# A SwiGLU feed-forward kernel: the first 256 rows of x loaded as row pairs, and the first gate weights issued from another queue

## The chip, the cores and the metric

The kernel runs on one core of a Trainium2 chip. The metric is device time in microseconds (us), from launch to end. The profile is one execution taken by the hardware profiler; its "span" runs from the core's first to its last instruction. PE is TensorE (PEld its weight loads), ACT is ScalarE, DVE is VectorE, POOL is GpSimd, and SP is SyncE, which only issues DMA here. DMA issued from SP is seen in the profile as queue q1, from ACT as q10, from POOL as q0.

## What is computed

x has 2048 rows of 640, the gate and up weights are 640 x 1536, the down weight is 1536 x 640, all bf16:

```
g = silu(x @ w_gate)
u = x @ w_up
out = (g * u) @ w_down
```

## The kernel before

The rows of x are worked on in four blocks of 512 (`S_BLK`), and the 1536 columns of the hidden layer in 12 pieces of 128 (`KF`, index `fc`). The contraction of 640 is 5 pieces of 128 (`KD`, index `kd`). In a block, each `fc` has five matmuls into `pg` (gate) and five into `pu` (up); ACT applies Silu from `pg`, DVE multiplies with `pu` and writes the hidden activations, transposed, into `aT`. When the 12 pieces are done, the down projection runs in two parts: output columns 512 to 639 come from one group of 12 matmuls `po_t`, with the 512 rows of the block as the moving side, so that they come out transposed; and columns 0 to 511 come from four groups `po_a`, one for each 128 rows `j`. `po_t` is copied by ACT to `ot_t` (L283), turned by DVE in 32x32 squares (L285) and stored from ACT's queue (L287). `po_a` is copied by ACT (L312) and stored from SP's queue (L321). The last four rows of x are handled apart, as row products on DVE (L148), which the change doesn't touch.

TensorE needs x with its columns on the partitions (`xT`). For most rows that is done by the DMA (`turn_x`, L110). For the first two chunks of 128 rows, `PE_X = 2`, it is done on TensorE: the rows are loaded into `x_sb` (L86), transposed against an identity (L190), and copied to `xT` by ACT (`kd` 0 and 1) and DVE (`kd` 2 to 4) (L195). Chunk 0 is loaded from SP's queue, chunk 1 from ACT's.

Behind these two loads come the first 256 columns (`fc` 0 and 1) of the gate and up weights, each in two parts, split at `K_CUT = 2`: `kd` 0 and 1 of the gate from SP, `kd` 2 to 4 of the gate from ACT, `kd` 0 and 1 of up from POOL, `kd` 2 to 4 of up from SP (L120). Then SP issues the transposing load of rows 256 to 511 and all the other weights.

`head()` writes TensorE's first work by hand, and `keep_order` keeps it so: 20 warming matmuls on a tile of ones (L177), ten transposes (five for each chunk), 14 gate matmuls (L240: for `kd` 0 and 1 first the 128 rows of chunk 0, then those of chunk 1, then `kd` 2 to 4 over both chunks' 256 rows), ten up matmuls over the same 256 rows, and then rows 256 to 511 of the same two pieces. After that the regular loop goes on with `fc` 2. Each engine works through its own instructions in the order given and waits at each for its semaphores.

Of the kernel before, what the change touches and what calls it, by code (L numbers as in the profile page):

```python
# [10 lines left out]
def _body(  # L11
# [8 lines left out]
    nc = tc.nc  # L20
    P = nc.NUM_PARTITIONS
# [8 lines left out]
    x2 = x.rearrange("b s d -> (b s) d")  # L30
    out2 = out.rearrange("b s d -> (b s) d")

    KD = D // P
    KF = F // P
    S_BLK = 512
# [7 lines left out]
    PE_X = 2  # L43
    K_CUT = 2
# [12 lines left out]
    x_sb = consts.tile([P, PE_X, D], bf16)  # L57
    xT = consts.tile([P, KD, S], bf16)
    wg_sb = consts.tile([P, KD, F], bf16)
    wu_sb = consts.tile([P, KD, F], bf16)  # L60
# [9 lines left out]

    make_identity(nc, ident[:])

    x_v = x2.rearrange("(c p) d -> p c d", p=P)
    xt_v = x2.rearrange("s (kd p) -> s kd p", p=P)
    wg_v = w_gate.rearrange("(kd p) f -> p kd f", p=P)
    wu_v = w_up.rearrange("(kd p) f -> p kd f", p=P)
    wd_v = w_down.rearrange("(kf p) d -> p kf d", p=P)

    def wslice(a, b):
        return slice(a * P, b * P)  # L80

    def load_w(eng, dst, src, a, b):
        eng.dma_start(out=dst[:, :, wslice(a, b)], in_=src[:, :, wslice(a, b)])

    def load_x(eng, c0, c1):
        eng.dma_start(out=x_sb[:, c0:c1, :], in_=x_v[:, c0:c1, :])  # L86

    def issue_order(a, b):
        tc.add_manual_dep(
# [18 lines left out]
    def turn_x(c0, c1):  # L108
        s_sl = slice(c0 * P, c1 * P)
        nc.sync.dma_start_transpose(out=xT[:, :, s_sl], in_=xt_v[s_sl])  # L110

    load_x(nc.sync, 0, 1)
    load_x(nc.scalar, 1, 2)
    f_sl = wslice(*W_CHUNKS[0])
    for dst, src, first, second in (
        (wg_sb, wg_v, nc.sync, nc.scalar),
        (wu_sb, wu_v, nc.gpsimd, nc.sync),
    ):
        for eng, k_sl in ((first, slice(0, K_CUT)), (second, slice(K_CUT, KD))):
            eng.dma_start(out=dst[:, k_sl, f_sl], in_=src[:, k_sl, f_sl])  # L120
    turn_x(PE_X, SUB)
    nc.scalar.activation(silu_first[:], ones[:, 0:1], ACT.Silu)
    for a, b in W_CHUNKS[1:]:
# [6 lines left out]
    def turn_w(dst, src):  # L130
# [7 lines left out]
        out=x_row[:],  # L138
        in_=x2[S - T : S, :].rearrange("t d -> (t d)").partition_broadcast(P),
# [29 lines left out]
    def do_dots(n):  # L169
        for _ in range(n):  # L170
            next(dots, None)
# [3 lines left out]
    def warm(n):  # L175
        for _ in range(n):
            nc.tensor.matmul(  # L177
                pw[:, 0:P],
                lhsT=ones[:].broadcast_to([P, P]),
                rhs=ones[:].broadcast_to([P, P]),  # L180
                start=True,
                stop=True,
            )

    def transpose_chunk(c, parts):
        c_sl = slice(c * P, (c + 1) * P)
        for copy, tag, k0, k1 in parts:
            pt = psum.tile([P, k1 - k0, P], bf16, tag=tag, name="pt")
            for kd in range(k0, k1):
                nc.tensor.transpose(  # L190
                    out=pt[:, kd - k0, :],
                    in_=x_sb[:, c, kd * P : (kd + 1) * P],
                    identity=ident[:],
                )
            copy(out=xT[:, k0:k1, c_sl], in_=pt[:])  # L195

    def proj(ps, w_sb, fc, sb, c0, c1):
        for kd in range(KD):
            nc.tensor.matmul(  # L199
                ps[:, c0:c1],  # L200
                lhsT=w_sb[:, kd, fc * P : (fc + 1) * P],
                rhs=xT[:, kd, sb * S_BLK + c0 : sb * S_BLK + c1],
                start=(kd == 0),
                stop=(kd == KD - 1),
            )

    def gu_tiles():
        pg = psum.tile([P, S_BLK], f32, tag="gu", name="pg", bufs=4)
        pu = psum.tile([P, S_BLK], f32, tag="gu", name="pu", bufs=4)
        return pg, pu  # L210

    def gate(pg, pu, sb, fc, n_s):

        s0 = sb * S_BLK
        sg = work.tile([P, S_BLK], f32, name="sg")
        nc.scalar.activation(sg[:, 0:n_s], pg[:, 0:n_s], ACT.Silu)  # L216
        nc.vector.tensor_tensor(  # L217
            out=aT[:, fc, s0 : s0 + n_s], in0=sg[:, 0:n_s], in1=pu[:, 0:n_s], op=ALU.mult
        )

    def head():

        dve, act = nc.vector.tensor_copy, nc.scalar.copy
        split = [(act, "po_a", 0, 2), (dve, "po_b", 2, KD)]
        late = PE_X * P
        (pg0, pu0), (pg1, pu1) = gu_tiles(), gu_tiles()  # L230
        warm(N_WARM)
        transpose_chunk(0, split)
        transpose_chunk(1, split)
        early = [(kd, c * P, (c + 1) * P) for c in range(PE_X) for kd in range(K_CUT)]
        early += [(kd, 0, late) for kd in range(K_CUT, KD)]
        for kd, c0, c1 in early:
            for fc, pg in ((0, pg0), (1, pg1)):


                nc.tensor.matmul(  # L240
                    pg[:, c0:c1],
                    lhsT=wg_sb[:, kd, wslice(fc, fc + 1)],
                    rhs=xT[:, kd, c0:c1],
                    start=(kd == 0 and c0 == 0),
                    stop=(kd == KD - 1),
                )
        proj(pu0, wu_sb, 0, 0, 0, late)
        proj(pu1, wu_sb, 1, 0, 0, late)
        for fc, pg, pu in ((0, pg0, pu0), (1, pg1, pu1)):
            proj(pg, wg_sb, fc, 0, late, S_BLK)  # L250
            proj(pu, wu_sb, fc, 0, late, S_BLK)
            gate(pg, pu, 0, fc, S_BLK)
        keep_order(mybir.EngineType.PE)
        keep_order(mybir.EngineType.Activation)
        keep_order(mybir.EngineType.Pool)

    head()
    for sb in range(NSB):
        n_s = S_BLK if sb < NSB - 1 else S_BLK - T
        for fc in range(KF):  # L260
            if sb == 0 and fc < 2:
                continue
            pg, pu = gu_tiles()
            proj(pg, wg_sb, fc, sb, 0, n_s)
            proj(pu, wu_sb, fc, sb, 0, n_s)
            gate(pg, pu, sb, fc, n_s)
            if sb > 0 and fc < KF - 2:
                do_dots(2)


        n_t = (SUB if sb < NSB - 1 else SUB - 1) * P
        po_t = psum.tile([P, n_t], f32, tag="po_b", name="po_t")
        for kf in range(KF):
            nc.tensor.matmul(  # L274
                po_t[:],
                lhsT=wd_sb[:, kf, DA:D],
                rhs=aT[:, kf, sb * S_BLK : sb * S_BLK + n_t],
                start=(kf == 0),
                stop=(kf == KF - 1),
            )  # L280
        ot_t = outp.tile([P, n_t], bf16, name="ot_t")
        ot_q = outp.tile([P, n_t], bf16, name="ot_q")
        nc.scalar.copy(ot_t[:], po_t[:])  # L283
        do_dots(3)
        nc.vector.transpose(out=ot_q[:], in_=ot_t[:])  # L285
        for q in range(P // Q):
            nc.scalar.dma_start(  # L287
                out=out2[
                    sb * S_BLK : sb * S_BLK + n_t, DA + q * Q : DA + (q + 1) * Q
                ].rearrange("(i r) c -> r i c", r=Q),  # L290
                in_=ot_q[q * Q : (q + 1) * Q, :].rearrange("r (i c) -> r i c", c=Q),
            )

        for j in range(SUB):
            s0 = sb * S_BLK + j * P
            last = sb == NSB - 1 and j == SUB - 1
            cols = [(0, DA, "po_a")]
            if last:
                cols = [(0, DA // 2, "po_a"), (DA // 2, DA, "po_a"), (DA, D, "po_b")]
            for c0, c1, tag in cols:  # L300
                po = psum.tile([P, c1 - c0], f32, tag=tag, name="po_a")
                for kf in range(KF):
                    nc.tensor.matmul(  # L303
                        po[:],
                        lhsT=aT[:, kf, s0 : s0 + P],
                        rhs=wd_sb[:, kf, c0:c1],
                        start=(kf == 0),
                        stop=(kf == KF - 1),
                    )
                ot = outp.tile([P, c1 - c0], bf16, name="ot" if c1 < D else "ot_b")  # L310
                if c1 < D:
                    nc.scalar.copy(ot[:], po[:])  # L312
                    eng = nc.sync
                else:
                    nc.vector.tensor_copy(out=ot[:], in_=po[:])  # L315
                    eng = nc.sync
                if 0 < j and not last:
                    do_dots(3)
                if sb == NSB - 1 and j == ROW_J:
                    row_tail()  # L320
                eng.dma_start(out=out2[s0 : s0 + P, c0:c1], in_=ot[:])  # L321
        if sb == 0:
            turn_x(2 * SUB, 3 * SUB)
            turn_w(wuT, wut_v)
            turn_x(3 * SUB, 4 * SUB)
# [107 lines left out]
```

## Time and profile before

| | us |
|---|---|
| median of 3 runs | 163.5 (163.18 to 163.65) |
| the profiled execution: its time | 163.61 |
| its span | 162.2 |
| PE busy (share of the span) | 159.8 (98%) |
| DVE busy | 110.8 (68%) |
| ACT busy | 42.9 (26%) |
| DMA, share of the chain that ended last | 2% |

The chain of waits is read from the last instruction backwards; in it PE has 97% of the span and the load of `x_sb` at the start has 1.7%. A busy TensorE says nothing of its pace: how many matmuls of what width went by in a stretch has to be counted. What lies around the span is 163.61 - 162.2 = 1.4 us.

### The profile page before, as it was taken

How to read it: one execution, taken by the hardware profiler on the slowest of the kernel's cores; microseconds unless marked ns; L12 is line 12 of the kernel's file. 1: busy time of each engine (PE TensorE's matmuls, PEld its weight loads, DVE VectorE, ACT ScalarE, POOL GpSimd, SP SyncE). 2: the span in 40 equal slices, each digit the busy share in tenths (PEclk: the TensorE clock that was granted, in tenths of full speed). 3: DMA queues.
4: the chain of work that ended last, by engine and by line, in shares of the span. 5: the costliest groups of instructions: out<-in, count | busy, mean ns of one | idle time of the engine just before them, and what ended most of it. 6: DMA issues, size and time to landing. Idle time of an engine off the chain costs nothing.

```text
span 162.2 us, 2119 instructions
## 1 busy us (share of the span) xinstructions
PE 159.8 (98%) x798; PEld 78.1 (48%) x798; DVE 110.8 (68%) x249; ACT 42.9 (26%) x74; POOL 1.5 (1%) x7
## 2 busy tenths in 40 slices
PE   8999999999999999999999999999999999999995
PEld 8854444444444444444444444444444444445454
DVE  1042233599469999979919999979964999993000
ACT  5132222112222222221222322221214222222121
POOL 3000000000000000000000000000000000000000
PEclk9999999999999999999999999999999999999999
DMA  7999999993179996003110000000320000000212
GB/s 215 275 343 350 363 217 220 240 216 87 35 164 161 205 177 136 4 0 34 65 65 0 0 4 2 0 0 1 63 68 33 0 0 0 0 0 4 50 39 73
DMA packets 42217, 15.86 MB, mean 98 GB/s; under 512 B 33216, under 2 KB 42048, under 8 KB 42208
## 3 DMA queue, kind: packets, MB, share of 16 engines
q1 hardware_dynamic: 33680, 14.75, 37.6%
q10 hardware_dynamic: 8480, 0.85, 3.4%
q8 instruction: 6, 0.10, 0.3%
q0 software_dynamic: 48, 0.13, 0.2%
q14 instruction: 3, 0.02, 0.1%
HBM read 6.88 MB, written 2.62 MB: 59 GB/s over the span
## 4 chain that ended last, share of the span: by engine, by line
PE 97%; DMA 2%; DVE 0%; issue 0%
PE pu L199 32%; PE pg L199 31%; PE po_a L303 26%; PE po_t L274 6%; DMA x_sb<-in_x_dram 2%; PE pg L240 1%; PE pt L190 1%; DVE ot_b L315 0%
## 5 line engine op out<-in xcount | busy, mean ns | idle before, releaser
L199 PE MATMUL pu<-xT,wu_sb 128*128 128x512 bf16 (+2 forms) x250 | 59.7, 370 | 0.0
L199 PE MATMUL pg<-xT,wg_sb 128*128 128x512 bf16 (+2 forms) x240 | 58.5, 374 | 0.0
L217 DVE TENSOR_TENSOR aT<-sg,pu 128x512 bf16<-128x512 f32 (+1 forms) x48 | 32.8, 684 | 32.4 <-PE pu L199 28.1
L216 ACT ACTIVATE sg<-pg 128x512 f32<-128x512 f32 (+1 forms) x48 | 28.6, 597 | 70.8 <-PE pg L199 66.2
L303 PE MATMUL po_a<-wd_sb,aT 128*128 128x512 bf16 (+2 forms) x216 | 42.8, 358 | 0.0
L148 DVE SCALAR_TENSOR_TENSOR prod<-wgT,x_row 128x640 f32<-128x640 bf16 x48 | 39.4, 821 | 1.1
L148 DVE SCALAR_TENSOR_TENSOR prod<-wuT,x_row 128x640 f32<-128x640 bf16 x48 | 39.4, 822 | 1.0
L199 PEld LDWEIGHTS <-wu_sb 128*128 128x128 bf16 x250 | 24.5, 98 | 27.3
L199 PEld LDWEIGHTS <-wg_sb 128*128 128x128 bf16 x240 | 23.5, 98 | 26.9
L303 PEld LDWEIGHTS <-aT 128*128 128x128 bf16 x216 | 20.7, 98 | 21.6
L312 ACT CAST ot<-po_a 128x512 bf16<-128x512 f32 (+1 forms) x17 | 9.5, 561 | 32.0 <-PE po_a L303 20.9
L274 PE MATMUL po_t<-aT,wd_sb 128*128 128x512 bf16 (+1 forms) x48 | 10.4, 366 | 0.0
L274 PEld LDWEIGHTS <-wd_sb 128*128 128x128 bf16 x48 | 4.7, 98 | 5.1
L315 DVE CAST ot_b<-po_a 128x128 bf16<-128x128 f32 x1 | 0.3, 292 | 9.9 <-PE po_a L303 9.9
L283 ACT CAST ot_t<-po_t 128x512 bf16<-128x512 f32 (+1 forms) x4 | 2.2, 559 | 11.6 <-PE po_t L274 11.6
L148 DVE DVE_READ_ACCUMULATOR prod<-wuT,x_row 128x1 f32 x48 | 4.0, 83 | 0.0
L148 DVE DVE_READ_ACCUMULATOR prod<-wgT,x_row 128x1 f32 x48 | 3.9, 82 | 0.0
L285 DVE STREAM_TRANSPOSE ot_q<-ot_t 128x512 bf16<-128x512 bf16 (+1 forms) x4 | 2.7, 678 | 1.7 <-ACT ot_t L283 1.7
L195 DVE COPY xT<-pt 128x384 bf16<-128x384 bf16 x2 | 0.7, 358 | 3.5 <-PE pt L190 3.5
L177 PE MATMUL pw<-ones 128*128 128x128 bf16 x20 | 2.3, 310 | 0.3 <-DVE ones L106 0.3
L240 PE MATMUL pg<-xT,wg_sb 128*128 128x128 bf16 (+1 forms) x14 | 2.2, 347 | 0.0
L177 PEld LDWEIGHTS <-ones 128*128 128x128 bf16 x20 | 2.0, 144 | 0.3 <-DVE ones L106 0.3
(16 smaller groups left out, 8.4 us busy)
## 6 DMA issues: line engine op xcount, KB each, us to landing
wd_sb<-in_w_down_dram SPq DMA_DIRECT2D x1, 1920.0 KB, 14.0
out_dram<-ot SPq DMA_DIRECT2D x15, 128.0 KB, 1.7
wg_sb<-in_w_gate_dram SPq DMA_DIRECT2D x2, 640.0 KB, 8.2
wu_sb<-in_w_up_dram SPq DMA_DIRECT2D x2, 640.0 KB, 8.8
x_row<-in_x_dram SPq DMA_DIRECT2D x1, 640.0 KB, 5.2
out_dram<-ot_q ACTq DMA_DIRECT2D x12, 32.0 KB, 1.9
wg_sb<-in_w_gate_dram SPq DMA_DIRECT2D x1, 320.0 KB, 4.4
wu_sb<-in_w_up_dram SPq DMA_DIRECT2D x1, 320.0 KB, 4.9
```

The source lines that it names most:

```text
L148: nc.vector.scalar_tensor_tensor(out=prod[:], in0=wT[:, fc, :], scalar=1.0, in1=x_row[:, t, :], op0=ALU.mult, op1=ALU.mult, accum_out=acc[ ...
L177: nc.tensor.matmul(pw[:, 0:P], lhsT=ones[:].broadcast_to([P, P]), rhs=ones[:].broadcast_to([P, P]), start=True, stop=True,)
L190: nc.tensor.transpose(out=pt[:, kd - k0, :], in_=x_sb[:, c, kd * P : (kd + 1) * P], identity=ident[:],)
L199: nc.tensor.matmul(ps[:, c0:c1], lhsT=w_sb[:, kd, fc * P : (fc + 1) * P], rhs=xT[:, kd, sb * S_BLK + c0 : sb * S_BLK + c1], start=(kd == 0 ...
L216: nc.scalar.activation(sg[:, 0:n_s], pg[:, 0:n_s], ACT.Silu)
L217: nc.vector.tensor_tensor(out=aT[:, fc, s0 : s0 + n_s], in0=sg[:, 0:n_s], in1=pu[:, 0:n_s], op=ALU.mult)
L240: nc.tensor.matmul(pg[:, c0:c1], lhsT=wg_sb[:, kd, wslice(fc, fc + 1)], rhs=xT[:, kd, c0:c1], start=(kd == 0 and c0 == 0), stop=(kd == KD ...
L274: nc.tensor.matmul(po_t[:], lhsT=wd_sb[:, kf, DA:D], rhs=aT[:, kf, sb * S_BLK : sb * S_BLK + n_t], start=(kf == 0), stop=(kf == KF - 1),)
L283: nc.scalar.copy(ot_t[:], po_t[:])
L285: nc.vector.transpose(out=ot_q[:], in_=ot_t[:])
L303: nc.tensor.matmul(po[:], lhsT=aT[:, kf, s0 : s0 + P], rhs=wd_sb[:, kf, c0:c1], start=(kf == 0), stop=(kf == KF - 1),)
L312: nc.scalar.copy(ot[:], po[:])
```

## The change

The 256 rows are loaded by one DMA from SP's queue. Partition p gets rows 2p and 2p+1, which lie together in memory (2560 bytes), where before it got rows p and 128+p by two DMAs of 1280 bytes a partition. So "chunk" 0 now holds the even rows among the first 256, and chunk 1 the odd ones, and so do the first 256 columns of `xT` and `aT`. The weights' parts are dealt out anew: gate `kd` 0 and 1 is ACT's first DMA, gate `kd` 2 to 4 and up `kd` 3 and 4 are SP's, up `kd` 2 is ACT's second, and up `kd` 0 and 1 stays with POOL. The order of the rows is put right at the output: in the first block ACT's copy of `po_t` is split in two, and the one for the first 256 columns writes with a stride; the stores of `po_a` for `j` 0 and 1 go to every second row.

```diff
-    load_x(nc.sync, 0, 1)
-    load_x(nc.scalar, 1, 2)
+    paired = PE_X * P
+
+    def paired_rows(ap):
+        return ap[0:paired, :].rearrange("(p c) d -> p c d", c=PE_X)
+
+    nc.sync.dma_start(out=x_sb[:], in_=paired_rows(x2))
     f_sl = wslice(*W_CHUNKS[0])
-    for dst, src, first, second in (
-        (wg_sb, wg_v, nc.sync, nc.scalar),
-        (wu_sb, wu_v, nc.gpsimd, nc.sync),
+    for eng, dst, src, a, b in (
+        (nc.scalar, wg_sb, wg_v, 0, K_CUT),
+        (nc.sync, wg_sb, wg_v, K_CUT, KD),
+        (nc.gpsimd, wu_sb, wu_v, 0, K_CUT),
+        (nc.scalar, wu_sb, wu_v, K_CUT, K_CUT + 1),
+        (nc.sync, wu_sb, wu_v, K_CUT + 1, KD),
     ):
-        for eng, k_sl in ((first, slice(0, K_CUT)), (second, slice(K_CUT, KD))):
-            eng.dma_start(out=dst[:, k_sl, f_sl], in_=src[:, k_sl, f_sl])
+        eng.dma_start(out=dst[:, a:b, f_sl], in_=src[:, a:b, f_sl])
...
-        nc.scalar.copy(ot_t[:], po_t[:])
+        plain = 0
+        if sb == 0:
+            plain = paired
+            nc.scalar.copy(
+                ot_t[:, 0:paired].rearrange("d (p c) -> d c p", c=PE_X),
+                po_t[:, 0:paired].rearrange("d (c p) -> d c p", c=PE_X),
+            )
+        nc.scalar.copy(ot_t[:, plain:n_t], po_t[:, plain:n_t])
...
+            rows = out2[s0 : s0 + P, :]
+            if s0 < paired:
+                rows = paired_rows(out2)[:, j, :]
...
-                eng.dma_start(out=out2[s0 : s0 + P, c0:c1], in_=ot[:])
+                eng.dma_start(out=rows[:, c0:c1], in_=ot[:])
```

Elsewhere the diff only renames `late` to `paired`. TensorE's matmuls, their shapes and their order are the same in both kernels.

More of the change, by code (lines that the diff above doesn't have):

```diff
@@ L71, in _body @@
     make_identity(nc, ident[:])
-    x_v = x2.rearrange("(c p) d -> p c d", p=P)
     xt_v = x2.rearrange("s (kd p) -> s kd p", p=P)
@@ L83, in load_w @@
         eng.dma_start(out=dst[:, :, wslice(a, b)], in_=src[:, :, wslice(a, b)])
-    def load_x(eng, c0, c1):
-        eng.dma_start(out=x_sb[:, c0:c1, :], in_=x_v[:, c0:c1, :])
     def issue_order(a, b):
@@ L228, in head @@
         split = [(act, "po_a", 0, 2), (dve, "po_b", 2, KD)]
-        late = PE_X * P
         (pg0, pu0), (pg1, pu1) = gu_tiles(), gu_tiles()
@@ L234, in head @@
         early = [(kd, c * P, (c + 1) * P) for c in range(PE_X) for kd in range(K_CUT)]
-        early += [(kd, 0, late) for kd in range(K_CUT, KD)]
+        early += [(kd, 0, paired) for kd in range(K_CUT, KD)]
         for kd, c0, c1 in early:
@@ L246, in head @@
                 )
-        proj(pu0, wu_sb, 0, 0, 0, late)
-        proj(pu1, wu_sb, 1, 0, 0, late)
+        proj(pu0, wu_sb, 0, 0, 0, paired)
+        proj(pu1, wu_sb, 1, 0, 0, paired)
         for fc, pg, pu in ((0, pg0, pu0), (1, pg1, pu1)):
-            proj(pg, wg_sb, fc, 0, late, S_BLK)
-            proj(pu, wu_sb, fc, 0, late, S_BLK)
+            proj(pg, wg_sb, fc, 0, paired, S_BLK)
+            proj(pu, wu_sb, fc, 0, paired, S_BLK)
             gate(pg, pu, 0, fc, S_BLK)
```

## The prediction, made before the changed kernel ran

> **What bounds the kernel now.** I read the chain of waits first, over its first 12 us and its end.
>
> ```profile
> 0.00 2.77 DMA x_sb<-in_x_dram
> 2.77 0.05 issue
> 2.81 1.25 PE pt L190 x10
> 4.06 1.99 PE pg L240 x14
> 6.05 1.09 PE pu L199 x10
> 7.14 0.55 PE pg L199 x5
> ```
>
> ```profile
> 157.96 2.32 PE po_a L303 x27
> 160.28 0.02 issue
> 160.31 0.29 DVE ot_b L315
> ```
>
> Columns: start, length, what; first the beginning, then the end. The first 2.77 us are the load of chunk 0; from 2.81 to 160.28 there is nothing but TensorE, piece after piece, with no wait between. So only two things can move the end: when TensorE starts on x, and how fast it goes. The stretches show both.
>
> ```profile
> 2.62:2.81 0.19, 0.00 (x0) 0.00 (x1) 0.00 (x0) 0.00 (x0) 0.00 (x0) 1.00 0.95 282
> 2.81:5.78 2.97, 2.97 (x24) 2.66 (x25) 0.72 (x2) 0.75 (x2) 0.00 (x0) 1.00 1.16 288
> 5.78:7.14 1.36, 1.36 (x14) 1.23 (x13) 0.00 (x0) 0.00 (x0) 0.00 (x0) 1.00 1.09 275
> ```
>
> After the stretch and its length come PE, PEld, DVE, ACT and POOL (busy us, instructions), then the granted clock. TensorE idles 0.19 us between warming and transposes. The granted clock reads 1.00 throughout, but the pace doesn't. The chain over 5.0 to 5.5 us gives:
>
> ```profile
> 4.92 0.64 PE pg L240 x3
> ```
>
> That is 213 ns for each matmul over 256 columns; the ten of the same width at 6.05 take 1.09 us, 109 ns each. TensorE goes at half its pace until about 5.8 us, warming included, and at full pace after that.
>
> **Part 1, the load of x.** Removed: two DMAs of 160 KB; added: one of 320 KB; and the gate's 128 KB now leave ACT's queue first. The issues and their times to landing before:
>
> ```profile
> wg_sb<-in_w_gate_dram ACTq DMA_DIRECT2D x1, 192.0 KB, 3.7
> wu_sb<-in_w_up_dram SPq DMA_DIRECT2D x1, 192.0 KB, 4.5
> x_sb<-in_x_dram SPq DMA_DIRECT2D x1, 160.0 KB, 2.8
> x_sb<-in_x_dram ACTq DMA_DIRECT2D x1, 160.0 KB, 3.0
> wg_sb<-in_w_gate_dram SPq DMA_DIRECT2D x1, 128.0 KB, 3.2
> wu_sb<-in_w_up_dram POOLq DMA_DIRECT2D x1, 128.0 KB, 4.2
> ```
>
> Chunk 0 landed at 2.77; chunk 1, issued at 0.13, at 0.13 + 3.0 = 3.13, just before its first transpose (the sixth, 2.81 + 5 x 0.107 = 3.34, its weights a little before). Chunk 1 cost nothing. Now TensorE's first transpose waits for both halves. DMA over the first 2.4 us:
>
> ```profile
> DMA packets 315, 0.33 MB, mean 139 GB/s; under 512 B 27, under 2 KB 315, under 8 KB 315
> ...
> q1 hardware_dynamic: 190, 0.19, 35.3%
> q10 hardware_dynamic: 125, 0.15, 16.9%
> ```
>
> All queues together had moved 0.33 MB by 2.4 us, the size of the new load. Lower bound: nothing else is served before x, its last packet starts by 2.4 as chunk 0's did, it lands at 2.77: no change. Upper bound: it lands as chunk 1 did, 3.13, and all the 128 KB of gate weights from ACT's queue go in between, at the 288 GB/s of the stretch above 0.45 us: 3.6. I take 3.15: the same 320 KB as the two loads before, on the same engines, with the gate's pieces beside it then as now. TensorE starts 0.05 later, at 3.2, as it did after 2.77: 0.4 us later than before (0 to 0.8).
>
> The Trainium skill, "DMA: Bandwidth & Descriptors", sections "Issuing engines are not separate DMA queues" and "Queues, rings and completion order", speaks against the change: whatever engine issues, the same 16 DMA engines serve all and take turns between queues by packets. By that rule the gate's early issue is paid for by x, toward the 3.6 end; 0.33 MB from q1 and q10 together in the row above agrees, but how they take turns no row shows.
>
> **What 0.4 us at the start are worth at the end.** The delay falls in the slow stretch, where 0.4 us of TensorE hold only 0.2 us of work at full pace. If full pace still begins at 5.8 us, the end moves by half: +0.2 us (0 to +0.4). If it waits for a set time of work on x, the end moves by all: +0.4 (0 to +0.8). I take the first: slow pace already held through warming, before any x, so nothing ties its end to x. The Trainium skill, "TensorE: Matmul & The Clock Gate", "Part 1: The HAM clock gate", says that the clock opens after a busy window of about 3.4 us, free-running, and is halved by idleness. The half pace agrees; that the window is free-running no single trace can show.
>
> **Part 2, the weights.** A delay of TensorE only helps them. Gate `kd` 2 to 4 landed at 0.56 + 3.7 = 4.3 and is needed by the ninth matmul of L240, 3.85 + 8 x 0.107 = 4.7; behind it up landed at 1.02 + 4.2 = 5.2 and 0.91 + 4.5 = 5.4, needed at 5.9 and 6.1; the transposing load of rows 256 to 511 landed at 1.42 + 5.0 = 6.4, needed at 7.0. The total ahead of each is as before: gate `kd` 2 to 4 now stands behind x on SP's queue, 320 + 128 + 192 KB in all, the same 640 KB as before. Gate `kd` 0 and 1 leaves ACT at 0.13 where it left SP at 0.45. Zero; without this cover, 0.1 us of lateness costs 0.05 to 0.1. Issue time: SP has 0.39 + 0.45 + 0.42 us where it had 0.39 + 0.42 + 0.47, ACT 0.42 + 0.39 against 0.40 + 0.45, so the transposing load and the table load behind them move by 0.05 us at most; each DMA still waits on nothing, and there are three on SP ahead of the transposing load, as before.
>
> **Part 3, the output.** ACT's rows:
>
> ```profile
> L312 ACT CAST ot<-po_a 128x256 bf16<-128x256 f32 x2 | 0.7, 372 | 1.7 <-PE po_a L303 1.7
> L283 ACT CAST ot_t<-po_t 128x512 bf16<-128x512 f32 x3 | 1.8, 586 | 9.2 <-PE po_t L274 9.2
> ```
>
> One copy of 586 ns becomes two of 372: +0.16 us of ACT, once. No row shows a write with a stride; bounds: no cost, or the copy at twice its time, +0.37; I take none, since the elements are as many, and L312 and L283 differ by their count alone. Behind it on ACT are four stores, issued from 34.90 to 36.88, and the copy of `po_a` `j` 0 at 36.92, which end by 0.16 to 0.53 later. TensorE needs that buffer again at `j` 2, at 33.50 + 2 x 2.59 = 38.7, and the copy ended at 37.5: 1.2 us of cover, so zero. DVE waits for `ot_t` 0.16 us longer, its row products behind; TensorE's next wait on DVE is a block away. The stores of `j` 0 and 1 write the same 1024 bytes a row, at another step; they land some 120 us before the end.
>
> **Sum.** Against the profiled execution: 163.61 (span 162.2 and 1.4 around it) + 0.2 + 0 + 0 = 163.8. That execution is 0.1 above the median; against the median, 163.5 + 0.2 = 163.7. Differences under 0.3%, 0.5 us, are about what a measurement can't tell from none.
>
> **Rivals.**
>
> - *The idle gap sets the slow pace back* (slower). Place: TensorE between the last warming matmul (2.62) and the first transpose. Before it idles 0.19 us, then 0.58. If that is enough to count as rest, full pace comes not at 5.8 but as long after the restart as it came after the first warming matmul, 5.78 - 0.30 = 5.48 us: at 8.7. The slow stretch is 2.9 us longer, half of that lost: +1.45 + 0.2 = +1.65, 165.2. It decides from the gap at which TensorE counts as idle, somewhere above 0.19 us. Against it: the gap of 0.19 cost nothing visible and 0.58 is a small part of the stretch. The Trainium skill's page on the clock gate asks for a whole idle window of about 3.4 us to halve the clock, but by its busy window an opening can also be missed and come 3.4 us later, an estimate of +1.7 from that page alone. Chance 0.15.
> - *The shift comes through whole, or x is at its late end.* +0.4 to +0.8, 163.9 to 164.3; for it, the taking of turns; against it, chunk 1's landing beside the gate's pieces. Chance 0.18.
> - *The load is hidden anyway*: packets of twice the size go faster, x lands by 2.77 or up to 0.15 earlier (TensorE isn't free before 2.62). -0.1 to +0.1, 163.4 to 163.6. For it: in the first packets the rate is far under the later 282 GB/s, so fewer, larger ones could start better. The gain can't go beyond 0.19, since warming stands before it. Chance 0.11.
> - *Full pace comes earlier by its own phase*: three runs of one program lie 0.47 us apart, which is 0.94 us of slow stretch. More than 0.5 us faster, near 162.9: chance 0.06.
>
> **How the numbers follow.** The forecast, x at about 3.15 and half of 0.4 us at the end, has 0.50, its own range 163.4 to 164.0: time 163.7. Faster by over 0.3% is the last rival and a little beside it: 0.07. Slower: the set-back, 0.15, and of the second rival with the tail of the forecast 0.14: 0.29. Within 0.3%: 0.64. The range holds the forecast, the second and third rival and most of the set-back: 163.1 to 165.2.
>
> **What would show it.** In the changed profile: `x_sb` lands once, at 2.9 to 3.5; the first `pt` starts 0.05 behind it; transposes and L240 run without a gap at 107 ns; 256-column matmuls change from 213 to 109 ns at about 5.8; first `pu` regular piece (9.33 before) is 0.2 later; the end of the last `po_a` moves by the same; two ACT copies in the first block and no TensorE wait at `j` 2. It is wrong if `x_sb` lands by 2.7, if the change of pace comes over 0.5 us away from 5.8, or if TensorE idles after its start on x.

## The result, and the profile after

The changed kernel takes 163.9 us in the median of 22 runs (163.31 to 165.63), the kernel before 163.41 (163.03 to 163.93). The ratio is 1.0036, 95% interval 1.0019 to 1.0054: 0.59 us slower (0.31 to 0.88), where +0.2 was forecast; the two medians lie 0.49 apart. Single runs of one and the same program differ by as much as the change does, which is a part of the answer. The profiled execution took 163.97 us, its span is 162.6.

The PE timeline of the changed kernel (start, length, line and operation, count, idle time before and its releaser), and from the same view of the kernel before the rows that answer to the second and third:

```profile
3.23 1.19 PE L192 MATMUL pt<-ident,x_sb 128*128 128x128 bf16 x10 [0.60 <-DMA x_sb<-in_x_dram]
4.25 1.42 PE L241 MATMUL pg<-xT,wg_sb 128*128 128x128 bf16 x14
5.51 1.25 PE L201 MATMUL pu<-xT,wu_sb 128*128 128x256 bf16 x10
```

```profile
3.85 2.20 PE L240 MATMUL pg<-xT,wg_sb 128*128 128x128 bf16 x14
5.89 1.25 PE L199 MATMUL pu<-xT,wu_sb 128*128 128x256 bf16 x10
```

TensorE starts on x 0.41 us later, as forecast (3.2). But the same 14 gate matmuls take 1.42 us in place of 2.20: full pace came at about 4.2 us in this execution, not at 5.8. The late start was more than won back by 5.51, where up starts (before: 5.89). Then it was lost again; the chain of waits of the changed kernel from 8 us on:

```profile
3.78 5.69 DMA wg_sb<-in_w_gate_dram
9.47 0.04 issue
9.52 0.39 PE pg L201
```

TensorE reached hidden piece 2 at 8.8 and its gate weights (columns 256 to 511) landed at 9.47: a wait of 0.73 us that the kernel before, with the same weights at 3.33 + 4.4 = 7.7 and TensorE there at 9.2, didn't have. The issues on SP's queue of the changed kernel, and behind them the first of the two as it was before:

```profile
1.45 2.29 SPq L106 DMA_TRANSPOSE xT<-in_x_dram  x1
3.78 0.58 SPq L82 DMA_DIRECT2D wg_sb<-in_w_gate_dram  x1
```

```profile
1.42 1.86 SPq L110 DMA_TRANSPOSE xT<-in_x_dram  x1
```

SP is held 2.29 us by the transposing load (1.86 before), so these weights leave 0.45 us later than in that profile. The rest of the lateness isn't issue: 12 of the 16 DMA engines had brought their part by 7.6, the other four took until 8.9 to 9.5. A smaller wait, 0.14 us, stands before the fifth gate matmul (4.61): ACT's copy of the second chunk to `xT` ends at 4.56, and the early full pace gets there first.

The output part, on ACT:

```profile
33.90 0.45 ACT L287 CAST ot_t<-po_t 128x256 bf16<-128x256 f32 x1 [3.07 <-PE po_t L275]
34.21 0.37 ACT L291 CAST ot_t<-po_t 128x256 bf16<-128x256 f32 x1
36.10 2.00 ACTq L295 DMA_DIRECT2D out_dram<-ot_q  x4
```

The strided copy takes 0.45 us beside 0.37 for the plain one, and both overlap; TensorE waits nowhere behind them in this execution.

**An account that closes.** Every profiled execution can be added up from the starts of its matmuls: when TensorE starts on x; what the half pace costs (the spacing of starts beyond 55.6, 109 and 215.7 ns for 128, 256 and 512 columns, which is what the traces show at full pace); waits beyond that (a double spacing of 432 ns is a missing record, and counted as two). What is left to the start of the last matmul is 155.82 us in the first profile of both kernels, and within 0.05 of it in all that follow. From there to the run's time it is 3.56 us in both. ("Old deal" and "new deal" stand for the weights' parts dealt out as in the kernel before and as in the changed one; fc 2 is hidden piece 2.)

| kernel | x (first half) lands | start on x | idle before it | full pace from | half pace costs | waits | sum of the three |
|---|---|---|---|---|---|---|---|
| before | 2.8 | 2.81 | 0.40 | 5.8 | 1.42 | 0 | 4.23 |
| before, again | 2.8 | 2.80 | 0.38 | 6.1 | 1.55 | 0 | 4.35 |
| changed | 3.2 | 3.23 | 0.81 | 4.2 | 0.47 | 0.89 | 4.59 |
| changed, again | 3.2 | 3.23 | 0.81 | 5.3 | 0.96 | 0 | 4.19 |
| changed, third | 3.3 | 3.30 | 0.88 | 6.9 | 1.68 | 0 | 4.98 |
| pairs, two loads | 2.5 | 2.56 | 0.15 | 6.3 | 1.79 | 0 | 4.35 |
| one load, old deal | 2.8 | 2.84 | 0.42 | 5.4 | 1.14 | 0.08 | 4.06 |
| one load, old deal, again | 2.8 | 2.87 | 0.46 | 5.2 | 1.07 | 0.06 | 4.00 |
| x alone | 3.2 | 3.21 | 0.80 | 6.4 | 1.52 | 0.63 | 5.36 |
| split, new deal | 2.3 | 2.42 | 0 | 4.6 | 0.78 | 1.67 | 4.87 |
| fc 2 from ACT | 3.3 | 3.37 | 0.96 | 7.4 | 1.81 | 0.24 | 5.42 |
| before, 16 warming | 2.3 | 2.33 | 0.35 | 4.2 to 4.7 | 0.82 | 0.72 | 3.87 |
| changed, 26 warming | 3.3 | 3.34 | 0.28 | 4.3 | 0.45 | 0.64 | 4.44 |
| changed, 28 warming | 3.1 | 3.21 | 0 | 3.2 | 0 | 0.71 | 3.92 |

(Times in us. Idle is counted from where the next matmul could have started, 2.41 after 20 warming matmuls.) The moment of full pace is read to about 0.1 us. A row is one execution; the medians of each kernel stand with its experiment.

### The profile page after: what moved, and what is told of

It reads as the page before. It is cut to its first block, busy times and chain, and to the rows that moved or that the text cites. A ratio compares the mean times of both kernels' runs of the same rounds, so it can differ in the third digit from the quotient of the medians.

```text
span 162.6 us, 2108 instructions
## 1 busy us (share of the span) xinstructions
PE 158.5 (98%) x786; PEld 77.3 (48%) x798; DVE 110.8 (68%) x249; ACT 43.0 (26%) x75; POOL 1.5 (1%) x7
## 3 DMA queue, kind: packets, MB, share of 16 engines
HBM read 6.88 MB, written 2.62 MB: 58 GB/s over the span
## 4 chain that ended last, share of the span: by engine, by line
PE 93%; DMA 3%; SPq 2%; issue 1%; DVE 0%
PE pu L201 30%; PE pg L201 30%; PE po_a L314 26%; PE po_t L275 6%; DMA wg_sb<-in_w_gate_dram 3%; SPq L106 1%; SPq L122 1%; SPq L113 0%; DVE ot_b L326 0%
## 5 line engine op out<-in xcount | busy, mean ns | idle before, releaser
L291 ACT CAST ot_t<-po_t 128x512 bf16<-128x512 f32 (+2 forms) x4 | 2.0, 506 | 8.6 <-PE po_t L275 8.6
L192 PE MATMUL pt<-ident,x_sb 128*128 128x128 bf16 x10 | 1.2, 305 | 0.6 <-DMA x_sb<-in_x_dram 0.6
```

Source lines behind the costliest of these rows:

```text
L291: nc.scalar.copy(ot_t[:, plain:n_t], po_t[:, plain:n_t])
```

## The experiments

### The kernels themselves, again

No edit. The changed kernel, twice, and the kernel before:

> The changed kernel once more, for a second profile. Head theory: x lands at 3.2 again, TensorE starts on x at 3.2, and the moment of full pace (4.2 us in the first profile of it, 5.7 in that of the kernel before) moves freely; the ratio is that of the result, 1.002 to 1.005. Late-weights theory: gate columns 256 to 511 land at 9.3 to 9.5 again and TensorE waits 0.5 to 0.9 us before hidden piece 2. Rival, a chance event of the first profile: they land at 7.8 to 8.3, tight over all 16 DMA engines, and TensorE doesn't wait.

> The changed kernel a third time, beside the three others of this job on one chip. By size theory x lands at 3.1 to 3.35 and TensorE starts on x 0.4 to 0.9 us after the kernel before; ratio 1.001 to 1.005. The end should again be the sum of start, slow-pace loss, waits and about 155.8 us of work.

> The kernel before itself, for a second profile. Ratio 1.000. Theory of scatter: its first half of x lands anywhere from 2.3 to 2.8 (2.77 in the first profile, 2.29 and 2.52 in two kernels with the same two loads), full pace comes at another time than 5.8, and the end is again start + slow-pace loss + waits + 155.8. Rival: 2.77 and 5.8 are fixed, within 0.05 and 0.2.

The changed kernel: 163.94 beside 163.43 us in the medians, ratio 1.0011 (0.9986 to 1.0036); and 164.08 beside 163.42, 1.0045 (1.0017 to 1.0073). The kernel before: 0.9996 (0.9981 to 1.0011). x lands where it did: 3.2, 3.2 and 3.3 in the three profiles of the one, 2.8 in both of the other. That doesn't refute the theory of scatter for the landing: the kernel before with 16 warming matmuls has the same loads, and there the first half landed at 2.3. The moment of full pace was another each time: 4.2, 5.3 and 6.9 in the one, 5.8 and 6.1 in the other. The weights of piece 2 were late on some engines again (8.5 and 9.3, and 8.95 in the kernel before), but of these only the execution with the early full pace was there before them: that wait is not the change's alone. (Two more with full pace by 4.6, "split, new deal" and "26 warming", waited 0.4 us in the same place; the one with 28 warming matmuls didn't.) SP's transposing load took 2.29, 2.11 and 2.20 us in the changed kernel, 1.86 and 2.12 in the one before, so its share is 0.2 us or so of later issue.

Over the three jobs (series of runs, each beside runs of the kernel before) 6 of the changed kernel's 46 runs lie at 165.0 to 165.6, beside 2 of the 127 runs of the kernel before that stand beside all experiments and the result. None of the six was profiled.

### Pairs by two loads

```diff
-    nc.sync.dma_start(out=x_sb[:], in_=paired_rows(x2))
+    for c, eng in ((0, nc.sync), (1, nc.scalar)):
+        eng.dma_start(out=x_sb[:, c, :], in_=paired_rows(x2)[:, c, :])
```

The weights' parts are dealt as in the kernel before.

> Row pairs and the changed output kept; x_sb loaded by two DMAs as before (even rows from SP, odd rows from ACT) and the weights' parts dealt as before. If the output part costs nothing and the load is the whole loss: ratio 1.000 (0.999 to 1.001), TensorE starts on x at 2.8. If the output part (a strided copy, stores to every second row) has a price: 1.002 or more, with a TensorE wait at the first block's down projection or a longer copy at 34 us.

163.60 beside 163.43 us, ratio 1.0006 (0.9997 to 1.0015). Its chain of waits at the start:

```profile
0.30 2.32 PE pw L178 x20
2.62 1.19 PE pt L191 x10
```

No load of x stands in it: in this execution the even rows landed at 2.5, before the end of warming that this view gives (2.62), and TensorE started on x at 2.56 and not at the 2.8 expected. The row order put right at the output costs nothing that can be measured (at most 0.15%).

### One load, the weights' parts dealt as before

```diff
-    for eng, dst, src, a, b in (
-        (nc.scalar, wg_sb, wg_v, 0, K_CUT),
...
+    for dst, src, first, second in (
+        (wg_sb, wg_v, nc.sync, nc.scalar),
+        (wu_sb, wu_v, nc.gpsimd, nc.sync),
+    ):
```

> One load of row pairs as in the change, the weights' parts dealt as before (gate kd 0 and 1 from SP behind x, kd 2 to 4 from ACT at once). If the single load is the cause, whatever stands beside it: x lands at 3.1 to 3.3, ratio 1.002 to 1.005 as in the result. If the gate's early issue from ACT is what delays x: with 192 KB from ACT in its place x lands just as late or later, 3.2 to 3.4. If only the new deal costs (later weights): ratio 1.000 to 1.001.

> One load of row pairs with the weights' parts dealt as before, a second time. If its landing at 2.79 was chance within the scatter of landings and the load's size decides: x lands at 3.1 to 3.35 here, and its ratio is within 0.001 of the changed kernel's in this job. If gate kd 0 and 1 from ACT's queue matter by themselves: x lands by 2.9 again and the ratio is 0.0015 or more below the changed kernel's.

163.64 beside 163.43 us, 1.0014 (1.0002 to 1.0026); again, 163.92 beside 163.42, 1.0043 (1.0013 to 1.0072), as much as the changed kernel in the same job. Beside the kernel before, one load is enough for a loss, and 2 of its 24 runs lie above 165; beside the pairs by two loads (1.0006, up to 1.0015) the first of the two intervals overlaps. Yet the row of its load (KB, us to landing) says:

```profile
x_sb<-in_x_dram SPq DMA_DIRECT2D x1, 320.0 KB, 2.8
```

Both times x landed at 2.8, the same 320 KB that take 3.2 us beside the new deal: the landing went by one theory and the time by the other. Why is open: the two profiled executions took 163.43 and 163.40 us, among the fastest of their kernel.

### x alone

```diff
-        (nc.scalar, wg_sb, wg_v, 0, K_CUT),
+        (nc.sync, wg_sb, wg_v, 0, K_CUT),
         (nc.sync, wg_sb, wg_v, K_CUT, KD),
         (nc.gpsimd, wu_sb, wu_v, 0, K_CUT),
-        (nc.scalar, wu_sb, wu_v, K_CUT, K_CUT + 1),
-        (nc.sync, wu_sb, wu_v, K_CUT + 1, KD),
+        (nc.sync, wu_sb, wu_v, K_CUT, KD),
```

> The changed kernel with nothing issued from ACT's queue at the start: x as one load of row pairs from SP, behind it on SP gate kd 0 and 1, gate kd 2 to 4, up kd 2 to 4; up kd 0 and 1 from POOL. If turn-taking with ACT's pieces holds x back: x lands at 2.6 to 2.85 and TensorE starts there. If the size alone does (320 KB where the first transpose waited for 160 KB): x lands at 3.0 to 3.2 as with the changed kernel. The pieces behind it land later by up to one issue (0.45 us); the ratio is open, 1.000 to 1.006.

164.79 beside 163.63 us, 1.0083 (1.0058 to 1.0108). Its DMA issues:

```profile
x_sb<-in_x_dram SPq DMA_DIRECT2D x1, 320.0 KB, 3.2
...
wu_sb<-in_w_up_dram SPq DMA_DIRECT2D x1, 192.0 KB, 5.4
```

With nothing on ACT's queue, x lands no sooner. So it isn't turn-taking with pieces on ACT's queue that held x back. The changed kernel's own trace agrees: by 2.4 us SP's queue had moved 0.29 MB and ACT's 0.01. The prediction feared that turn-taking by the Trainium skill, "DMA: Bandwidth & Descriptors", "Queues, rings and completion order"; no run here bears it out for x. In this execution the pieces behind x are late too: up lands at 1.43 + 5.4 = 6.8 and rows 256 to 511 at 8.1, and TensorE waits for both (0.63). That this is the loss beyond the changed kernel's is likely, not shown; 4 of its 12 runs lie above 165 us.

### x split, the new deal kept

```diff
-    nc.sync.dma_start(out=x_sb[:], in_=paired_rows(x2))
+    for c in range(PE_X):
+        nc.sync.dma_start(out=x_sb[:, c, :], in_=paired_rows(x2)[:, c, :])
```

> The changed kernel with x split in two loads again, even rows and then odd rows, both from SP's queue; the weights' parts as in the change, gate kd 0 and 1 from ACT at once. If the joining of the loads is the cause (TensorE waits for 320 KB rather than 160): even rows land at 2.3 to 2.8, odd rows by 3.3 without a wait, ratio 1.000 to 1.001. If gate kd 0 and 1 from ACT at once is the cause: even rows land at 2.9 or later, ratio 1.002 to 1.004.

163.87 beside 163.63 us, 1.0018 (1.0005 to 1.0032). Its PE timeline:

```profile
2.42 0.74 PE L193 MATMUL pt<-ident,x_sb 128*128 128x128 bf16 x5
3.42 0.71 PE L193 MATMUL pt<-ident,x_sb 128*128 128x128 bf16 x5 [0.27 <-DMA x_sb<-in_x_dram]
```

The even rows land at 2.3 and TensorE starts as warming ends, so gate `kd` 0 and 1 from ACT doesn't delay them. The odd rows, second on SP, land at 3.4, and here TensorE waits in the middle. A fourth DMA ahead of the transposing load adds 0.5 us to all behind it, three more waits, 1.67 us in all in this execution. Neither theory had that.

### Gate weights of piece 2 from ACT

```diff
-        load_w(nc.sync, wg_sb, wg_v, a, b)
+        load_w(nc.scalar if a == 2 else nc.sync, wg_sb, wg_v, a, b)
         load_w(nc.sync, wu_sb, wu_v, a, b)
```

> The changed kernel with gate columns 256 to 511 issued from ACT, behind its table load (about 2.6 us), in place of from SP behind the transposing load (3.6 to 3.8 us). If late weights for hidden piece 2 carry a part of the loss: they land before 8 us, no wait at fc 2, ratio 1.001 or less. If they don't: they land early and the ratio stays at 1.003 to 1.004. A loss (1.005 or more, rows 256 to 511 landing after 7.0) would say that they take the place of the transposing load.

165.09 beside 163.63 us, 1.0083 (1.0056 to 1.0110). They left ACT at 1.2 us, not 2.6, and landed at 6.9; in return up `kd` 0 and 1 landed at 6.7, where TensorE waited 0.21, and rows 256 to 511 at 7.8. So it doesn't test late weights alone; it is the loss that was expected if they take the transposing load's place. Its PE timeline shows something else:

```profile
3.37 1.25 PE L192 MATMUL pt<-ident,x_sb 128*128 128x128 bf16 x10 [0.75 <-DMA x_sb<-in_x_dram]
4.41 2.34 PE L241 MATMUL pg<-xT,wg_sb 128*128 128x128 bf16 x14
6.75 1.57 PE L201 MATMUL pu<-xT,wu_sb 128*128 128x256 bf16 x10
```

Full pace came only at 7.4, after the longest idleness before x of all profiles, 0.96 us; 8 of its 12 runs lie over 164.9 us, one of them at 168.06.

### More and less warming

```diff
-    N_WARM = 20
+    N_WARM = 28
```

(and 26, in the changed kernel; 16 in the kernel before)

> The changed kernel with 26 warming matmuls in place of 20, so that TensorE is busy until about 3.25 and has no idle gap before x; x lands at 3.2 as before. If the gap delays full pace: ratio down to 1.001 to 1.002 and no runs above 165. If the gap has no say: ratio 1.003 to 1.005, and full pace starts anywhere between 2.9 and 6.3, as in the profiles so far.

> The changed kernel with 28 warming matmuls, which keep TensorE busy to 3.27, past the landing of x. If the idle 0.6 us before x delays full pace or brings the runs above 165: 0.001 to 0.002 below the changed kernel's ratio in this job and no run above 165. If the gap has no say: the same ratio within 0.001.

> The kernel before with 16 warming matmuls in place of 20: TensorE idles from 2.19 to 2.81, 0.62 us, as the changed kernel does (0.60), with nothing else changed; TensorE's start on x stays at 2.8. Set-back theory (idleness delays full pace): slower by 0.1 to 0.3% in the median, with single runs 1 to 2 us slower. If idleness has no say: ratio 1.000 (0.999 to 1.001) and the runs within 163.0 to 163.9.

With 26: 163.71 beside 163.63 us, 1.0007 (0.9992 to 1.0023). In its profile warming ended at 3.06, not 3.25, and x landed at 3.3, so 0.28 us of idleness were left. With 28: 163.76 beside 163.42, 1.0016 (0.9997 to 1.0035), where the changed kernel in the same job has 1.0045 (1.0017 to 1.0073). Both went the way that idleness matters, and 1 of the 24 runs lies above 165; the intervals still overlap, so the times alone don't settle it. The PE timeline with 28:

```profile
1.99 1.39 PE L179 MATMUL pw<-ones 128*128 128x128 bf16 x12
3.21 0.72 PE L192 MATMUL pt<-ident,x_sb 128*128 128x128 bf16 x10
3.94 1.32 PE L241 MATMUL pg<-xT,wg_sb 128*128 128x128 bf16 x14
```

Here the transposes themselves go at full pace, 0.72 us where they took 1.19 to 1.25 in the changed kernel: it came at 3.2, as no other profile shows it. In this execution TensorE also waited 0.16 us at the third `po_a` group, for a buffer that ACT copied late behind stores that held its queue for 3.0 us: the cover that the prediction put at 1.2 us is not always there. The kernel before with 16: 163.38 beside 163.43, 1.0009 (0.9990 to 1.0027). Two of its 12 runs lie above the 163.9 that was expected without a say of idleness (164.01 and 164.87). But its x landed at 2.3 in the profile, so the idleness was 0.35 us and not the 0.62 it was made for; it says nothing on the question.

## Why the prediction was right in kind and too small

**Right.** x landed at 3.2 (3.15 forecast), TensorE started 0.05 later. The bound was the load at the start and the pace; the last matmul's start is start + half pace + waits + 155.8 in all fourteen executions. The output part costs nothing that can be measured (1.0006, and the copies overlap). The kernel is slower, as forecast: 163.9 us where 163.7 was expected.

**The step that failed: "What 0.4 us at the start are worth at the end".** It took half of the 0.4 us, holding that full pace begins at 5.8 us whatever happens. One profile had shown one moment, and I made it a constant. In fourteen executions, of ten kernels, it lies anywhere from 3.2 to 7.4. In the changed kernel it came at 4.2, 5.3 and 6.9, where the prediction itself took a moment over 0.5 us away from 5.8 as a sign of being wrong; in its first profile TensorE also idled after its start on x, another such sign. That this execution (163.97) lies so near the 163.8 forecast for it is luck: beside the first profile of the kernel before, the start cost 0.41, the half pace 0.95 less and the waits 0.89 more, +0.36 in all, and only the start was in the sum. The last rival (full pace earlier by its own phase, chance 0.06) had the moving moment right, but not what the waits would take back. Idleness may have a say in the moment: the runs with more warming point that way, without settling it.

The Trainium skill, "TensorE: Matmul & The Clock Gate", "Part 1: The HAM clock gate", says that activity is judged in windows of about 3.4 us that run free of the program. No row here shows such a window; the moment moves over 4.2 us, more than one window, so by that page some executions missed one. Laying such a window before each moment gives an estimate from that page's length: the changed kernel's first profile reached full pace at 4.2 with 0.81 us of idleness in the window, 24% of it; "fc 2 from ACT" missed one that ended at 4.0 with 0.96 us, 28%; "pairs, two loads" missed one that ended at 2.9 with 0.30 before the first matmul and 0.15 before x outside warming, plus the 0.48 before the program began, 27%; with 28 warming matmuls one that ended at 3.2 and held 0.52, 15%, was taken. All fourteen fit a limit of about a quarter. But that limit is fitted to these executions, only the first three named press on it, and that TensorE counts as idle before the program began is taken and not shown.

What idleness would mean without the page: the idleness before x doubles, from 0.4 to 0.8 us. If TensorE must then be at work for about 0.4 us longer before full pace can come, the moment moves by the delay too, on average. Then the whole delay comes through, half of it as later work and half as later pace: +0.4 us where the forecast had +0.2. This is the second rival's price (chance 0.18), by another way than it was argued. It is argued and not shown: the profiled executions don't bear it out. There start and half pace together come to 4.29 us on average in the changed kernel (3.70, 4.19 and 4.98) and to 4.29 in the kernel before (4.23 and 4.35); they differ by the waits alone, 0.30 on average. Three and two executions are too few to show a mean.

The 0.4 itself may be too small. It counts from a landing at 2.8, and with two loads the first half also landed at 2.5 ("pairs") and 2.3 ("16 warming"). With 20 warming matmuls TensorE could then start at 2.41 at the earliest. Counted over these four, the changed kernel starts on x 0.6 us later, an estimate: half of that would be +0.3, all of it +0.6.

**The remaining 0.2 us** between +0.4 and the measured 0.59 (0.31 to 0.88) lie within the interval. Two more things may fill it. "A delay of TensorE only helps" the weights was wrong in one profile of three: the sum had the transposing load issued no more than 0.05 us later, but not that it would hold SP longer, so the weights of piece 2 left at 3.6 to 3.8 where it had been 3.3 and 3.6; when full pace comes early, TensorE reaches piece 2 before them, and the early pace is lost again (0.73 us). And the runs above 165 us raise the mean: without the three in the result, the mean of the changed kernel is 0.4 us above that of the kernel before, with them 0.6. The six of 46 are where the set-back rival put them, 165.2; but none was profiled, so their cause stays open.

**Open:** why the single load lands at 2.8 beside the old deal and at 3.2 otherwise, twice and seven times (3.1 to 3.3, "x alone" among them, which has neither deal), and why the landing at 2.8 brings no better times; what share each of late start, late pace and late weights has in the mean. No kernel here beat the kernel before.

## What to carry to other kernels

Where the engine that sets the end is fed by one first load, look first for the smallest piece that lets it start, before joining transfers: with two loads the first transpose waits for 160 KB, which landed at 2.3 to 2.8 us in five executions, and the second half mostly lands just before it is needed; the 320 KB landed at 2.8 to 3.3 in nine. A moment read from one profile is a sample; take a second profile of the same kernel before making it a constant in a sum. And add up the executions you have (start, slow pace, waits, a rest that must come out the same): it shows which term differs where times alone, at 0.3%, show little.

## What the runs showed of the hardware

Full pace of TensorE, which the granted clock didn't show (1.00 throughout, with matmuls of 128 columns 107 ns apart and then 55.6), came between 3.2 and 7.4 us after the first instruction in kernels with the same matmuls, and between 4.2 and 6.9 in three executions of one; each us of half pace is worth half a us at the end. Single DMA engines lag: the gate weights of piece 2 were on 12 engines by 7.6 us and on all 16 at 9.5 in one execution, on all by 7.8 in another. The first transposing load holds SP's queue for 1.75 to 2.51 us. What was issued ahead of it doesn't set that alone: with 640 KB ahead on SP it was 1.81 twice (one load, old deal) and 1.94 to 2.29 in the new deal, with 480 KB 1.75 to 2.12.
